# Channel attention over 384 x 384 x 384: VectorE sums 20 rows of a tile and TensorE's last rows wait for it

## The chip, the cores and the metric

One core of one Trainium2 chip. The time is device microseconds of that core. Three runs of the kernel before took 527.71, 527.98 and 530.86 us; their median is 527.98.

## What is computed

`x` is one image of 384 x 384 pixels with 384 channels in bf16 (113.2 MB), `w1d` a single weight. The mean of each channel over all pixels is multiplied by the weight and put through a sigmoid; every pixel is then multiplied by that vector of 384 gates.

```python
g = jnp.einsum("bhwc->bc", x) / (H * W)
s = _sigmoid(g * w1d[0])          # k = 1: the window has one tap
return x * s[:, None, None, :]
```

The image has to be read once and written once, 226.5 MB in all, and the gate of the first pixel depends on the last.

## The kernel before

The kernel doesn't read the image twice. It estimates the gate from the first four rows (`sum_early`, `s_early`), multiplies every tile by that estimate and stores it, while it sums the whole image on the side. At the end it computes the true gate (`s_true`) and compares the two as bf16 bit patterns. Where they differ anywhere (`redo`), a second pass loads, multiplies and stores everything again; otherwise it is skipped. For the reference's data it is skipped.

A "row" is one pixel for each of the 128 partitions: 128 x 384 values. There are 1152 rows, in 18 tiles of `TILE` = 64 rows (6.3 MB). SBUF holds `SLOTS` = 4 tiles; tile k lies in slot k mod 4, so the load of tile k waits until the store of tile k-4 has landed. Loads are issued by SP (some of the first four tiles' by ScalarE), stores by ScalarE. Both kinds of transfer run on the same 16 DMA engines.

A tile's work is split over two engines:

- **TensorE** sums the first 48 rows (`TILE - OWN`) by matmuls with a matrix of ones, 512 columns at a time, so 36 matmuls a tile, into three PSUM banks (`acc` of group 1). This is the loop of `sum_all`: for each tile it waits for the semaphore `ready`, then runs the first `FORE` = 32 rows and signals, then the other 16 and signals again. GpSimd does nothing but relay: when all of a tile's loads have landed it raises `ready` (L119, L467).
- **VectorE** sums the last `OWN` = 16 rows by one `reduce_sum` over the rows (`sum_own`, L338), adds that to `own` (L345), and then multiplies the whole tile in place by `s_early` (`put` and `gate`, L210). The product overwrites what TensorE reads, so it waits for TensorE's signal of that tile. Tile 0's product is cut in two at row `FORE`, so that its first part needs only TensorE's first signal.

The order of the work on each engine is that in which the function calls `plan.op` and `plan.dma`; the class `Planner` adds the semaphore waits from what each operation reads and writes. In the loop over k (L457) come, for each tile from the fifth on: VectorE's sum and product of tile k-4 and its store, then the load of tile k. Before the load of tile 4, ScalarE runs one long activation whose result nobody uses (`pause`, L399), so that this load starts some microseconds after the first store has landed. The last tile is multiplied first, into another slot, and summed afterwards (L474, L475).

At the end `join_own` splits `own` into three bf16 terms, which TensorE sums over the partitions into `acc_own`; `add_banks` adds the PSUM banks together in six VectorE operations; then come the true gate on ScalarE, the comparison, its maximum (`wrong`) and the cast to the integer `redo`. `second_pass` lets SP, ScalarE and VectorE read `redo` from SBUF and branch. After that block ScalarE waits for all 18 stores (L597), two in one instruction.

Of the kernel before, what the change touches and what calls it, by code (L numbers as in the profile page):

```python
# [3 lines left out]
P = 128  # L4
# [151 lines left out]

TILE, SLOTS, EARLY, LEAD, FORE, OWN = 64, 4, 4, 8, 32, 16


PAUSE = 9


def bass_standalone__channel_attn_eca__vision_kernel(
# [10 lines left out]
    def dram(view, r0, n):  # L176
# [4 lines left out]
    w_one = nc.alloc_sbuf_tensor("w_one", [1, 16], BF16)  # L181
    w_scaled = nc.alloc_sbuf_tensor("w_scaled", [P, 2], F32)
    warm = nc.alloc_sbuf_tensor("warm", [P, 2], F32)
    wrong = nc.alloc_sbuf_tensor("wrong", [P, 1], F32)
    redo = nc.alloc_sbuf_tensor("redo", [P, 1], I32)
    total = nc.alloc_sbuf_tensor("total", [P, C], F32)
    zeros = nc.alloc_sbuf_tensor("zeros", [P, 2], BF16)
    own = nc.alloc_sbuf_tensor("own", [P, C], F32)
    part = nc.alloc_sbuf_tensor("part", [P, C], F32)
    terms = nc.alloc_sbuf_tensor("terms", [P, 3 * C], BF16)  # L190
    n_arena = nc.sbuf_bytes_remaining // (2 * C)
    arena = nc.alloc_sbuf_tensor("arena", [P, n_arena * C], BF16)
    acc = [
        [nc.alloc_psum_tensor(f"acc{g}_{i}", [P, WIDE], F32) for i in range(3)]
        for g in range(2)
    ]
    w_all = nc.alloc_psum_tensor("w_all", [P, WIDE], F32)
    acc_own = nc.alloc_psum_tensor("acc_own", [P, WIDE], F32)

    def at(r0, n):  # L200
        assert r0 + n <= n_arena
# [9 lines left out]

    n_tiles = n_rows // TILE
    base = SLOTS * TILE
    assert n_rows % TILE == 0 and base + PAUSE <= n_arena
    assert EARLY % 4 == FORE % 4 == (TILE - OWN) % 4 == 0 and EARLY <= LEAD <= FORE
    last = n_tiles - 1
    ready = nc.alloc_semaphore("ready")

    def slot(k):
        return k % SLOTS * TILE  # L220
# [39 lines left out]
    def add_rows(e, group, column, n, start, stop):  # L260

        n_wide = n * C // WIDE
        all_of = [
            mm(
                e,
                acc[group][i % 3][:, :],
                ones[:],
                arena[:, column + i * WIDE : column + (i + 1) * WIDE],
                start and i < 3,
                stop and i >= n_wide - 3,  # L270
            )
            for i in range(n_wide)
        ]
        return all_of[-1]
# [9 lines left out]
    def nothing(e, bank, start):  # L284

        none = zeros[:, 0:1].broadcast_to([P, WIDE])
        return mm(e, acc[1][bank][:, :], ones[:], none, start, not start)

    def sum_all():

        def one(e, s):
            e.wait_ge(ready, 1).then_inc(ready, -1)  # L292
            for r, n in ((0, FORE), (FORE, TILE - OWN - FORE)):
                add_rows(e, 1, (slot(s) + r) * C, n, False, False).then_inc(
                    plan.sems["tensor"], 1
                )

        def emit(e):
            for i in range(3):
                nothing(e, i, True)  # L300
            rounds = -(-n_tiles // SLOTS)
            some = n_tiles - (rounds - 1) * SLOTS
            with e.Fori(0, rounds) as k:
                for s in range(some):
                    one(e, s)
                if some < SLOTS:
                    with e.If(k < rounds - 1):
                        for s in range(some, SLOTS):
                            one(e, s)
            for i in range(3):  # L310
                done = nothing(e, i, False)
            done.then_inc(plan.sems["tensor"], 1)

        plan.streams["tensor"].append(("block", emit, None))

    def add_banks(group, copy):

        for m, lo, hi in ((0, 0, C), (0, C, WIDE), (1, 0, 256), (1, 256, WIDE),
                          (2, 0, P), (2, P, WIDE)):
            c = (128 * m + lo) % C  # L320
            part = total[:, c : c + hi - lo]
            of = acc[group][m][:, lo:hi]
            if copy and (m, lo) == (0, 0):
                emit = lambda e, part=part, of=of: e.tensor_copy(part, of)  # L324
            else:
                emit = lambda e, part=part, of=of: e.tensor_tensor(  # L326
                    part, part, of, ALU.add
                )
            plan.op("vector", emit, reads=[f"acc{group}", "total"], writes=["total"])

    def sum_own(k):

        r0 = slot(k) + TILE - OWN
        view = at(r0, OWN).rearrange("p (t c) -> p c t", t=OWN)
        to = part if k else own
        plan.op(
            "vector",
            lambda e: e.reduce_sum(to[:], view, axis=mybir.AxisListType.X),  # L338
            reads=rows(r0, OWN),
            writes=["part" if k else "own"],  # L340
        )
        if k:
            plan.op(
                "vector",
                lambda e: e.tensor_tensor(own[:], own[:], part[:], ALU.add),  # L345
                reads=["own", "part"],
                writes=["own"],
            )

    def join_own():  # L350

        for i in range(3):
            term = terms[:, i * C : (i + 1) * C]
            plan.op(
                "vector",
                lambda e, term=term: e.tensor_copy(term, own[:]),  # L356
                reads=["own"],
                writes=[f"term{i}"],
            )
            if i < 2:  # L360
                plan.op(
                    "vector",
                    lambda e, term=term: e.tensor_tensor(  # L363
                        own[:], own[:], term, ALU.subtract
                    ),
                    reads=["own", f"term{i}"],
                    writes=["own"],
                )
        for i in range(3):
            term = terms[:, i * C : (i + 1) * C]  # L370
            plan.op(
                "tensor",
                lambda e, i=i, term=term: mm(
                    e, acc_own[:, :C], ones[:], term, i == 0, i == 2
                ),
                reads=["ones", f"term{i}"],
                writes=["acc_own"],
            )

    def put(place, n, r0, to=None, parts=None):  # L380
        to, i = place if to is None else to, 0
# [11 lines left out]

    def pause(r0):

        to = at(base, PAUSE)
        plan.op(
            "scalar",
            lambda e: e.activation(  # L399
                to, warm[:, 0:1].broadcast_to([P, PAUSE * C]), ACT_F.Sigmoid  # L400
            ),
            reads=["warm"],
            writes=rows(r0, 1) + ["pause"],
        )

    def weight():

# [22 lines left out]
            )  # L430

    plan.op("gpsimd", lambda e: e.memset(warm[:, 0:1], 0.0), writes=["warm"])
    plan.op("vector", lambda e: e.memset(ones[:], 1.0), writes=["ones"])  # L433
    plan.op("gpsimd", lambda e: e.memset(zeros[:], 0.0), writes=["zeros"])
    load(0, TILE, 0, hi=LEAD)
    plan.dma("sync", w_one[0:1, 0:1], w1d.unsqueeze(0), writes=["w_one"])
# [5 lines left out]
    heads = {e: len(plan.streams[e]) for e in ("sync", "scalar")}  # L442
    weight()
    sum_early()
    add_banks(0, copy=True)
    plan.op(
        "scalar",
        lambda e: e.activation(  # L448
# [5 lines left out]
    plan.need("tensor", ["zeros"])  # L454
    sum_all()

    for k in range(n_tiles):  # L457
        if k >= SLOTS:

            for i in range(2) if k == SLOTS else () if k < SLOTS + 2 else (k - SLOTS,):  # L460
                sum_own(i)
                put(slot(i), TILE, row0(i), parts=None if i else (FORE, TILE - FORE))
            if k == SLOTS:
                pause(slot(k))
            load(slot(k), TILE, row0(k), reads=["pause"] if k == SLOTS else ())
        there = rows(slot(k), TILE)
        plan.relay(ready, "gpsimd", "tensor", there, rows(slot(k), FORE), ["acc1"])  # L467
        plan.signals("tensor", rows(slot(k) + FORE, TILE - OWN - FORE), ["acc1"])
    plan.signals("tensor", [], ["acc1"])
    for k in range(n_tiles - SLOTS, last):  # L470
        sum_own(k)
        put(slot(k), TILE, row0(k))

    put(slot(last), TILE, row0(last), slot(n_tiles))  # L474
    sum_own(last)  # L475
    join_own()


    add_banks(1, copy=True)
    plan.op(  # L480
        "vector",
        lambda e: e.tensor_tensor(total[:], total[:], acc_own[:, :C], ALU.add),  # L482
        reads=["acc_own", "total"],
        writes=["total"],
    )
    plan.op(
        "scalar",
        lambda e: e.activation(  # L488
# [12 lines left out]
    )  # L501
    plan.op(
        "vector",
        lambda e: e.reduce_max(wrong[:], total[:], axis=mybir.AxisListType.X),  # L504
        reads=["total"],
        writes=["wrong"],
    )
    plan.op(
        "vector",
        lambda e: e.tensor_copy(redo[:], wrong[:]),  # L510
        reads=["wrong"],
        writes=["redo"],
    )
    checked = (plan.sems["vector"], plan.count["vector"])
# [5 lines left out]
    for k, n in enumerate(split(n_rows, half)):  # L520
        place = above + k % 2 * half
        again.dma("sync", at(place, n), dram(x_rows, r0, n), writes=rows(place, n))
        again.op(
            "vector",
            gate(place, place, n, s_true),
            reads=rows(place, n),
            writes=rows(place, n),
# [31 lines left out]
    with nc.Block() as block:  # L559
# [18 lines left out]
        @block.vector  # L578
        def _(e):
            plan.emit("vector", e)  # L580
            second_pass("vector", e)

        @block.scalar
        def _(e):
# [7 lines left out]
        @block.gpsimd  # L592
        def _(e):
            plan.emit("gpsimd", e)

    for token in plan.final:
        nc.scalar.wait_ge(*token)  # L597
# [28 lines left out]
```

## Time and profile before

The profiled execution took 527.94 us, with a span of 526.5 us from the first to the last instruction.

| | |
|---|---|
| runs | 527.71, 527.98, 530.86 us |
| profiled execution, its span | 527.94, 526.5 us |
| VectorE busy | 440.0 us (84%), 78 instructions |
| TensorE busy | 180.0 us (34%), 648 matmuls |
| ScalarE, GpSimd busy | 5.8 us, 0.3 us |
| DMA | 226.51 MB, mean 430 GB/s over the span |
| VectorE products (L210) | 17 of 12.95 us, two of 6.56 us |
| VectorE sums of 16 rows (L338) | 18, mean 10.5 us |
| VectorE adds of 128x384 f32 (L345) | 17 of 0.56 us |
| a load of one tile, issue to landing | 41.8 us (median) |
| a store of one tile, issue to landing | 49.9 us (median) |

A page of a profile gives each engine's busy time over the whole span, and the same in 40 slices of 13.2 us, one digit a slice, in tenths. A line of the timeline gives start and duration in us, engine, line of the code, operation, output and input with partitions and elements, and in brackets how long the engine stood idle before it and what released it. A line of the waits says who waited for whom: the total in us, the number of times, and the longest. A busy share says little by itself: an engine that has time to spare costs nothing, and one that is busy beside a slower one doesn't either.

### The profile page before, as it was taken

The numbers are of one execution on the slowest core, as the hardware profiler recorded it, in microseconds if no ns is written. First come the engines' busy times: TensorE is split into PE (matmuls) and PEld (weight loads), VectorE is DVE, ScalarE is ACT, GpSimd is POOL, SyncE is SP. The second block draws the span as 40 slices with busy tenths as digits, with TensorE's granted clock in tenths as the row PEclk, the third lists the DMA queues.
The fourth block names the chain that finished last, engine by engine and source line by source line (L and its number), as shares of the span: only waits on it lengthen the run. The fifth ranks groups of instructions, "written<-read, shape, count | busy, mean of one in ns | idle before, by whom it ended". The sixth has DMA issues, their size and how long they took to land.

```text
span 526.5 us, 902 instructions
## 1 busy us (share of the span) xinstructions
PE 180.0 (34%) x648; PEld 0.2 (0%) x2; DVE 440.0 (84%) x78; ACT 5.8 (1%) x5; POOL 0.3 (0%) x6
## 2 busy tenths in 40 slices
PE   2255752043240707061422506070513315070701
PEld 0000000000000000000000000000000000000000
DVE  1869999999996978969696969789696969698795
ACT  1000020000000000000000000000000000000000
POOL 0000000000000000000000000000000000000000
PEclk9996967558585858567575858576675858585765
DMA  9999999999999999999999999999999999999998
GB/s 375 433 459 405 418 448 448 418 418 467 429 418 418 467 429 418 429 459 426 418 429 459 426 418 441 445 429 418 448 437 429 418 459 429 426 418 459 429 426 359
DMA packets 5620, 226.51 MB, mean 430 GB/s; under 512 B 626, under 2 KB 626, under 8 KB 754
## 3 DMA queue, kind: packets, MB, share of 16 engines
q10 hardware_dynamic: 3024, 122.29, 53.7%
q1 hardware_dynamic: 2594, 104.20, 46.0%
q14 instruction: 2, 0.02, 0.0%
HBM read 113.25 MB, written 113.25 MB: 430 GB/s over the span
## 4 chain that ended last, share of the span: by engine, by line
DMA 42%; another core or an unknown queue 27%; DVE 21%; issue 7%; SPq 0%; ACT 0%; DVEq 0%
DMA arena<-in_x_dram 24%; DMA out_dram<-arena 18%; DVE part L338 12%; DVE arena L210 7%; DVE own L345 1%; DVE total L326 0%; SPq L109 0%; DVE own L363 0%; DVE terms L356 0%; ACT arena L488 0%; DVE total L496 0%; DVE total L482 0%; DVE wrong L504 0%; DVE total L324 0%
## 5 line engine op out<-in xcount | busy, mean ns | idle before, releaser
L248 PE MATMUL acc<-arena,ones 128*128 128x512 bf16 x637 | 176.1, 441 | 312.2 <-PEq L292 310.8
L210 DVE TENSOR_TENSOR arena<-arena,s_early 128x24576 bf16<-128x24576 bf16 (+1 forms) x19 | 233.2, 12278 | 11.5 <-PE acc L248 6.5
L338 DVE TENSOR_REDUCE part<-arena 128x384 f32<-128x6144 bf16 x17 | 179.2, 10539 | 56.9 <-DMA arena<-in_x_dram 56.9
L338 DVE TENSOR_REDUCE own<-arena 128x384 f32<-128x6144 bf16 x1 | 10.4, 10435 | 0.6 <-DMA arena<-in_x_dram 0.6
L345 DVE TENSOR_TENSOR own<-own,part 128x384 f32<-128x384 f32 x17 | 9.5, 558 | 0.6
L425 DVE TENSOR_SCALAR w_scaled<-w_all 128x1 f32<-128x1 f32 x2 | 0.2, 152 | 8.0 <-PE w_all L416 8.0
L248 PE MATMUL acc_own<-terms,ones 128*128 128x384 bf16 x3 | 1.4, 479 | 15.3 <-DVE terms L356 15.3
L488 ACT ACTIVATE arena<-total,w_scaled 128x384 bf16<-128x384 f32 x1 | 0.6, 615 | 440.3 <-DVE total L482 440.3
L326 DVE TENSOR_TENSOR total<-total,acc 128x128 f32<-128x128 f32 (+2 forms) x10 | 3.9, 393 | 0.3
L399 ACT ACTIVATE arena<-warm 128x3456 bf16<-128x3456 f32 x1 | 3.1, 3082 | 61.9 <-DMA out_dram<-arena 61.9
L416 PE MATMUL w_all<-w_one,ones 1*128 1x1 bf16 x1 | 0.2, 158 | 9.3 <-DMA w_one<-in_w1d_dram 9.3
L248 PE MATMUL acc<-zeros,ones 128*128 128x512 bf16 x6 | 2.3, 507 | 0.0
L324 DVE COPY total<-acc 128x384 f32<-128x384 f32 x2 | 1.1, 554 | 1.2 <-PE acc L248 1.2
L410 ACT ACT_TABLE_LOAD x1 | 1.3, 1283 | 2.3 <-issue 2.3
L433 DVE MEMSET ones<- 128x128 bf16 x1 | 0.2, 165 | 1.3 <-PEq L611 1.3
L363 DVE TENSOR_TENSOR own<-own,terms 128x384 f32<-128x384 f32 x2 | 1.1, 559 | 0.1
L356 DVE CAST terms<-own 128x384 bf16<-128x384 f32 x3 | 1.1, 359 | 0.1
L496 DVE TENSOR_TENSOR total<-arena,s_early 128x384 f32<-128x384 uint16 x1 | 0.6, 558 | 0.7 <-ACT arena L488 0.7
L448 ACT ACTIVATE s_early<-total,w_scaled 128x384 bf16<-128x384 f32 x1 | 0.6, 614 | 9.8 <-DVE total L326 9.8
L482 DVE TENSOR_TENSOR total<-total,acc_own 128x384 f32<-128x384 f32 x1 | 0.6, 554 | 0.1
L246 PE MATMUL acc<-arena,ones 128*128 128x512 bf16 x1 | 0.6, 608 | 0.0
L504 DVE TENSOR_REDUCE wrong<-total 128x1 f32<-128x384 f32 x1 | 0.6, 553 | 0.0
(10 smaller groups left out, 1.2 us busy)
## 6 DMA issues: line engine op xcount, KB each, us to landing
out_dram<-arena ACTq DMA_DIRECT2D x18, 6144.0 KB, 49.9
arena<-in_x_dram SPq DMA_DIRECT2D x16, 6144.0 KB, 41.8
arena<-in_x_dram ACTq DMA_DIRECT2D x2, 3072.0 KB, 41.5
arena<-in_x_dram ACTq DMA_DIRECT2D x1, 2688.0 KB, 14.0
arena<-in_x_dram SPq DMA_DIRECT2D x1, 2688.0 KB, 21.4
arena<-in_x_dram SPq DMA_DIRECT2D x1, 768.0 KB, 7.8
w_one<-in_w1d_dram SPq DMA_DIRECT2D x1, 0.0 KB
```

What stands on the lines that cost most here:

```text
L210: return lambda e: e.tensor_tensor(to_v, v, s_b, ALU.mult)
L246: loaded.append(e.matmul(bank, weights, moving, start=start, stop=stop))
L248: return e.add_instruction(mybir.InstMatmult(name=nc.get_next_instruction_name(), engine=mybir.EngineType.PE, ins=[e.lower_ap(moving), e.l ...
L324: emit = lambda e, part=part, of=of: e.tensor_copy(part, of)
L326: emit = lambda e, part=part, of=of: e.tensor_tensor(part, part, of, ALU.add)
L338: lambda e: e.reduce_sum(to[:], view, axis=mybir.AxisListType.X),
L345: lambda e: e.tensor_tensor(own[:], own[:], part[:], ALU.add),
L356: lambda e, term=term: e.tensor_copy(term, own[:]),
L363: lambda e, term=term: e.tensor_tensor(own[:], own[:], term, ALU.subtract),
L399: lambda e: e.activation(to, warm[:, 0:1].broadcast_to([P, PAUSE * C]), ACT_F.Sigmoid),
L410: lambda e: e.activation(warm[:, 1:2], warm[:, 0:1], ACT_F.Sigmoid),
L448: lambda e: e.activation(s_early[:], total[:], ACT_F.Sigmoid, scale=w_scaled[:, 0:1]),
```

## The change

Six things are changed together.

1. `OWN` goes from 16 to 20 and `FORE` from 32 to 40. VectorE sums 20 rows of each tile; TensorE sums 44, of which 40 (30 matmuls) after `ready`.
2. TensorE's last 4 rows (3 matmuls) wait for a new semaphore, `summed`, which VectorE's sum of that tile raises. VectorE's product then needs one wait, for TensorE, which covers the reading of both engines.
3. A tile's sum isn't added to `own` at once. It goes to one of six places above the slots (`part(i)`, f32); after every fourth tile (4, 8, 12, 16) one `reduce_sum` over five places joins them, behind that tile's product. At the end the remaining two are joined into `own`.
4. The three PSUM banks of a group are one tensor, and one `reduce_sum` over its four pieces of 384 columns (`total_of`) takes the place of six operations. The three terms of `own` are added by TensorE into the first of these banks, so `acc_own` and its addition go.
5. The second pass multiplies on GpSimd, so GpSimd reads `redo` and VectorE no longer does. The maximum is written as an integer directly, without the cast. The memset of `ones` is on GpSimd.
6. The pause is three activations of 1152 columns rather than one of 3456.

```diff
-TILE, SLOTS, EARLY, LEAD, FORE, OWN = 64, 4, 4, 8, 32, 16
-PAUSE = 9
+TILE, SLOTS, EARLY, LEAD, FORE, OWN = 64, 4, 4, 8, 40, 20
+PARTS = 6
+PAUSE, PAUSES = 3, 3
...
-    acc = [
-        [nc.alloc_psum_tensor(f"acc{g}_{i}", [P, WIDE], F32) for i in range(3)]
-        for g in range(2)
-    ]
+    acc = [nc.alloc_psum_tensor(f"acc{g}", [P, 3 * WIDE], F32) for g in range(2)]
...
+    summed = nc.alloc_semaphore("summed")
...
         def one(e, s):
-            e.wait_ge(ready, 1).then_inc(ready, -1)
-            for r, n in ((0, FORE), (FORE, TILE - OWN - FORE)):
+            for of, r, n in ((ready, 0, FORE), (summed, FORE, TILE - OWN - FORE)):
+                e.wait_ge(of, 1).then_inc(of, -1)
                 add_rows(e, 1, (slot(s) + r) * C, n, False, False).then_inc(
                     plan.sems["tensor"], 1
                 )
...
-            for i in range(3):
-                done = nothing(e, i, False)
-            done.then_inc(plan.sems["tensor"], 1)
+            for i in (1, 2):
+                nothing(e, i, False)
...
-    def add_banks(group, copy):
...
+    def total_of(group):
+        view = acc[group][:, :].rearrange("p (t c) -> p c t", c=C)
+        plan.op(
+            "vector",
+            lambda e: e.reduce_sum(total[:], view, axis=mybir.AxisListType.X),
+            reads=[f"acc{group}"],
+            writes=["total"],
+        )
+
+    def part(i, n=1):
+        return at(base + 2 * i, 2 * n).bitcast(F32)
...
     def sum_own(k):
         r0 = slot(k) + TILE - OWN
         view = at(r0, OWN).rearrange("p (t c) -> p c t", t=OWN)
-        to = part if k else own
+        i = free[0]
+        free[0] += 1
+        reads, writes = rows(r0, OWN), part_rows(i)
+        for token in plan._needs(reads, writes):
+            plan._wait("vector", token)
+        plan.streams["vector"].append(
+            (
+                "op",
+                lambda e: e.reduce_sum(part(i), view, axis=mybir.AxisListType.X),
+                summed,
+                1,
+            )
+        )
+        plan._record(all_summed[k], reads, writes)
+        kept.append(i)
+
+    def join_parts(to=None):
+        lo, n = min(kept), len(kept)
+        assert sorted(kept) == list(range(lo, lo + n))
+        i = 0 if lo else PARTS - 1
+        view = part(lo, n).rearrange("p (t c) -> p c t", c=C)
+        out = part(i) if to is None else to[:]
         plan.op(
             "vector",
-            lambda e: e.reduce_sum(to[:], view, axis=mybir.AxisListType.X),
-            reads=rows(r0, OWN),
-            writes=["part" if k else "own"],
+            lambda e: e.reduce_sum(out, view, axis=mybir.AxisListType.X),
+            reads=part_rows(lo, n),
+            writes=["own"] if to is not None else part_rows(i),
         )
-        if k:
-            plan.op(
-                "vector",
-                lambda e: e.tensor_tensor(own[:], own[:], part[:], ALU.add),
-                reads=["own", "part"],
-                writes=["own"],
-            )
+        kept[:], free[0] = [i], 1
...
-                lambda e, i=i, term=term: mm(
-                    e, acc_own[:, :C], ones[:], term, i == 0, i == 2
-                ),
+                lambda e, term=term: mm(e, acc[1][:, :C], ones[:], term, False, False),
...
-        to = at(base, PAUSE)
+        to, of = terms[:, : PAUSE * C], warm[:, 0:1].broadcast_to([P, PAUSE * C])
+        for i in range(PAUSES):
...
-    plan.op("vector", lambda e: e.memset(ones[:], 1.0), writes=["ones"])
+    plan.op("gpsimd", lambda e: e.memset(ones[:], 1.0), writes=["ones"])
...
+    def put_tile(k):
+        sum_own(k)
+        put(slot(k), TILE, row0(k), parts=None if k else (FORE, TILE - FORE))
+        if len(kept) == PARTS - 1:
+            join_parts()
...
         plan.signals("tensor", rows(slot(k) + FORE, TILE - OWN - FORE), ["acc1"])
-    plan.signals("tensor", [], ["acc1"])
+        all_summed.append((plan.sems["tensor"], plan.count["tensor"]))
...
     put(slot(last), TILE, row0(last), slot(n_tiles))
     sum_own(last)
+    join_parts(own)
     join_own()
-    add_banks(1, copy=True)
-    plan.op(
-        "vector",
-        lambda e: e.tensor_tensor(total[:], total[:], acc_own[:, :C], ALU.add),
...
+    total_of(1)
...
-        lambda e: e.reduce_max(wrong[:], total[:], axis=mybir.AxisListType.X),
+        lambda e: e.reduce_max(redo[:], total[:], axis=mybir.AxisListType.X),
...
         again.op(
-            "vector",
+            "gpsimd",
             gate(place, place, n, s_true),
...
         def _(e):
             plan.emit("vector", e)
-            second_pass("vector", e)
...
         @block.gpsimd
         def _(e):
             plan.emit("gpsimd", e)
+            second_pass("gpsimd", e)
```

## The prediction

> **What bounds the kernel now.** I read the share of the DMA engines first, then the waits, then VectorE's own timeline, then the end. From the page, VectorE's and the DMA's rows over 40 slices:
>
> ```profile
> DVE  1869999999996978969696969789696969698795
> ...
> DMA  9999999999999999999999999999999999999998
> ```
>
> The DMA engines are never below nine tenths. VectorE has idle slices only from about 140 us on. The waits say for what, and what the loads wait for:
>
> ```profile
> DVE part L338 <- DMA arena<-in_x_dram: 56.9, 13, 5.3
> ```
>
> ```profile
> SPq L109 <- DMA out_dram<-arena: 364.1, 13, 28.8
> ```
>
> Thirteen times VectorE waits some 5 us for a tile to land, and a load is issued when the store that frees its slot has landed. So the middle is bound by bytes: 226.5 MB at 430 GB/s is the whole span, and a tile takes 29.0 us. VectorE's work for one tile, where it waits for nothing:
>
> ```profile
> 92.32 10.41 DVE L338 TENSOR_REDUCE part<-arena 128x384 f32<-128x6144 bf16 x1
> ...
> 102.76 0.56 DVE L345 TENSOR_TENSOR own<-own,part 128x384 f32<-128x384 f32 x1
> 103.24 12.95 DVE L210 TENSOR_TENSOR arena<-arena,s_early 128x24576 bf16<-128x24576 bf16 x1
> ...
> 116.11 10.51 DVE L338 TENSOR_REDUCE part<-arena 128x384 f32<-128x6144 bf16 x1
> ```
>
> From start to start 23.8 us: sum 10.44, add 0.48, product 12.87 (the records overlap by 0.08). VectorE has 5.2 us a tile to spare, and none of its work but the first tile's and the last's shows in the time. The end:
>
> ```profile
> 489.92 12.96 DVE L210 TENSOR_TENSOR arena<-arena,s_early 128x24576 bf16<-128x24576 bf16 x1 [5.04 <-DMA arena<-in_x_dram]
> ...
> 502.79 10.41 DVE L338 TENSOR_REDUCE part<-arena 128x384 f32<-128x6144 bf16 x1
> ...
> 521.28 0.15 DVE L510 CAST redo<-wrong 128x1 int32<-128x1 f32 x1
> ```
>
> ```profile
> L597 ACTq EVENT_SEMAPHORE  x9: 38/38/38, 523.2 to 526.4; - x9
> ```
>
> The last load lands at 489.9, its store is issued at 502.9 and lands 23.5 us later, at 526.4. Beside it VectorE ends the sum: the flag is written at 521.43, the engines read it and leave the block by 523.2, and ScalarE's nine waits for the stores begin; the trace's records have the eighth at 524.1, and only the ninth waits, until 526.4. So the flag's chain needs about 2.7 us after `redo` and has 2.3 us to spare. **Anything that makes VectorE's chain end more than 2.3 us later sets the time.** Span 526.5, run 527.94: 1.5 us lie around it, and that run stands 0.04 under the median.
>
> **What the Trainium skill says.** "VectorE: DVE Perf Modes", The perf-mode tier table: a reduce has only the 1x mode, a bf16 product reaches 2x. The trace agrees: the product takes 0.53 ns an element, the sum (10.42 - 0.15)/6144 = 1.67 ns (0.15 is what the one-column operations cost). The contiguous reduce of L504 takes (0.55 - 0.15)/384 = 1.05. "Advanced Engine Details and Errata", Memory Cachelines: touching another 16-byte line at each access costs; that fits 1.67 against 1.05, as the sum steps a row (768 bytes) at a time. "TensorE: Matmul & The Clock Gate", Part 1: after some 3.4 us idle the array runs at half clock, 427 against 216 ns for 512 columns. The trace agrees: granted clock 0.50 in 92 to 100 us where TensorE idles. "DMA: Bandwidth & Descriptors", Issuing engines are not separate DMA queues: both queues share 16 engines. The trace agrees: 434 GB/s in 461 to 490 us with loads and stores, 442 to 457 in 490 to 505 with stores alone.
>
> **The change, part by part.**
> *Rows.* VectorE sums 20 rows for 16: 7680 x 1.67 ns + 0.15 = 13.0 us, 2.56 more a tile. TensorE has 33 matmuls for 36; it idles half the time, worth nothing by itself.
> *The new wait.* The last 3 matmuls wait for VectorE's sum, and the product, which overwrites the tile, waits for them. Before, all 36 were done when the sum was (9.3 to 10.4 us against 10.5), so this wait was free. Now VectorE stands still for the hop to TensorE and three matmuls. The nearest row is the opening:
>
> ```profile
> 9.37 0.61 PE L246 MATMUL acc<-arena,ones 128*128 128x512 bf16 x1
> ...
> 9.77 1.06 PE L248 MATMUL acc<-arena,ones 128*128 128x512 bf16 x2
> ...
> 10.87 0.56 DVE L324 COPY total<-acc 128x384 f32<-128x384 f32 x1 [1.17 <-PE acc L248]
> ```
>
> Three matmuls at half clock, until the VectorE copy that waits for them starts: 1.50 us; with 0.1 for the hop there (load landing to TensorE's start is 0.13) 1.6. At full clock 3 x 0.22 + 0.2 = 0.85, the lower bound. I take 1.6: with VectorE as the pace, TensorE does the next tile's 30 matmuls during the product (some 8.5 us of 12.9) and then idles 17 us. Behind the waiting matmuls stand the next tile's 30, which have that product's time; who waits for the three is the product, and behind it the store and the load into that slot.
> *Joins.* 17 adds of 0.48 go. After tiles 4, 8, 12 and 16 a reduce of 5 parts (1920 f32, in steps of 1536 bytes), at the end one of 2. Not shown by the trace for f32: at 1.05 ns 2.2 and 0.95 us, at 1.67 ns 3.4 and 1.45. A third reading, that the sum is 16 cycles plus a fixed cost for each of its 384 outputs, gives 6.1 and 4.9 (and 12.0 for the sum of 20 rows). I take 1.67, since the steps are long too.
> *PSUM totals.* Copy and five adds (2.7 us) and the add of `acc_own` (0.6) become one reduce of 1536: 1.75, 2.75 or 5.7 us by the same three readings; I take 2.75. The first total's difference is hidden: the first product waits for TensorE at 31.08, `s_early` is there at 14.2.
> *FORE 40.* The first product waits for 30 matmuls, not 24: 6 x 0.22 = 1.3 us, at 32.4; tile 0's store goes out at 45.3, not 44.1.
> *Pause in three, memset of `ones` and second pass on GpSimd, the dropped cast.* The pause delays only the load of tile 4, which lands at 112 us and is wanted at 128. `ones` is wanted at 9.3. GpSimd reads the flag in VectorE's place (0.93 us there; unknown on GpSimd, -0.3 to +1.5, taken as 0). The cast is worth 0.15. SP's and ScalarE's transfers stay the same ones in the same order.
>
> **The sum.** One tile on VectorE becomes 13.0 + 1.6 + 12.9 = 27.5 us, with a join each fourth tile 28.3: under 29.0, but the cover is nearly gone, and VectorE starts late. Loads of the first tiles are there early (tile 4 at 112 us), and VectorE, done with tile 0 at 45.3, wants tile 5 at about 159 where it landed at 141; it never again meets a late load. Tiles 1 to 16: 45.3 + 16 x 27.5 + 4 x 3.4 = 498.9. The last load is there at 490, so the last product ends at 511.8, 9 us later than before. Then sum 13.0, wait for TensorE 1.6, join 1.45, casts and subtractions 2.35, two matmuls 0.9, total 2.75, ScalarE 0.7, the compare and the maximum 1.15: `redo` at 535.7. Flag 2.7: span 538.4, and 1.5 around it: **539.9 us**, 2.3% more. The last store, issued at 511.8, lands by 526.5: the DMA queue no longer sets the end. What is late next is VectorE's chain from 45 us on.
>
> **Rivals.**
> *Cover holds (not slower).* If the three matmuls run at full clock (0.85), tiles 1 to 16 end at 45.3 + 16 x 26.75 + 13.6 = 486.9, before the last load at 490. Then only the tail counts: 502.9 + 23.2 + 2.7 + 1.5 = 530.3, +0.4%. It decides from the point where the tile falls under 26.9. For it: records from 62.5 to 66 show that the clock stays up some 4 us after the last matmul. Against it: the idle time is 17 us once VectorE paces.
> *F32 reduces at 1.05 ns:* 4 x 1.2 + 0.5 + 1.0 less: 533.6, just on the edge.
> *Fixed cost per output:* 17 x 1.0 less for sums, 4 x 2.7 + 3.4 + 3.0 more for reduces: 540.
> *Stores starve.* A store is issued some 2 us before or after the previous one lands (20 us before, now). Then one queue works alone; 490 to 522 us shows no loss of rate, so I allow 5 us: 545.
> *Faster* than 1% would need fewer bytes or a higher rate; the DMA's 226.5 MB leave 2 us at most.
> *It doesn't do what it says:* if the product didn't wait for the three matmuls, it would be the first rival with 0: 529.4.
>
> **Numbers.** Forecast 0.47, cover holds or no wait 0.18, fast f32 0.20, cost per output 0.09, starved 0.04, faster 0.02. About 1% (533.3) is what a measurement of this kernel tells from no change. Half of the fast-f32 case is above it: slower 0.70, same 0.28, faster 0.02. Range 529.5 to 544.
>
> **What would show it.** The sum at 13.0; each product starting 1.6 after its sum, with TensorE as releaser; reduces of 128x1920 at 3.4; VectorE's waits for loads gone after tile 1; the last product near 499; the last of ScalarE's final waits no longer the late one. Waits of VectorE for loads that stay, or a gap under 1 us, would make the prediction wrong.

## The result, and the profile after

The changed kernel takes 536.74 us (median of six runs, 536.35 to 537.68), against 528.14 before: a ratio of 1.0156, with a 95% interval of 1.0134 to 1.0178. It is 8.6 us slower. The ratios here and below are the recorded ones; they differ from the quotients of the medians by up to 0.0014. The profiled execution took 536.56 us, with a span of 535.0.

From the page of the kernel after, the busy tenths of VectorE and of the DMA engines in 40 slices of 13.4 us:

```profile
DVE  1969898989898989899998989898989898989995
...
DMA  9999999999999999999999999999999999999992
```

From 40 us on VectorE is busy eight or nine tenths of every slice but the last; the deeper gaps that began at 140 us are gone. The DMA engines still look full, but in the last slice they are nearly done, and VectorE is not. The waits, in total, number of times and longest, name the new one:

```profile
DVE arena L206 <- PE acc L245: 29.7, 17, 4.3
...
DVE arena L353 <- DMA arena<-in_x_dram: 1.8, 1, 1.8
```

Before, 13 of VectorE's sums waited for a load, 57 us in all. Now one does, at tile 0, and 17 products wait for TensorE: tile 0's, which waited before too (6.5 us then, 4.3 now), and 16 new ones, 25.4 us together. One tile on the timeline (start, duration, engine, line):

```profile
185.33 12.97 DVE L353 TENSOR_REDUCE arena<-arena 128x384 f32<-128x7680 bf16 x1
...
198.41 8.67 PE L245 MATMUL acc<-arena,ones 128*128 128x512 bf16 x33 [18.70 <-PEq L295]
199.89 12.96 DVE L206 TENSOR_TENSOR arena<-arena,s_early 128x24576 bf16<-128x24576 bf16 x1 [1.59 <-PE acc L245]
212.76 12.97 DVE L353 TENSOR_REDUCE arena<-arena 128x384 f32<-128x7680 bf16 x1
```

The sum takes 12.97 us, then VectorE stands for 1.59 until TensorE has done three matmuls (the line of 33 is those three and the next tile's 30), then comes the product: 27.43 us from sum to sum. TensorE had been idle for 18.7 us before these three, and the clock granted to it while they run, from 198.4 to 199.9 us, is 0.50. The end of VectorE's chain:

```profile
497.47 12.95 DVE L206 TENSOR_TENSOR arena<-arena,s_early 128x24576 bf16<-128x24576 bf16 x1
510.34 12.97 DVE L353 TENSOR_REDUCE arena<-arena 128x384 f32<-128x7680 bf16 x1
...
529.22 1.76 DVE L322 TENSOR_REDUCE total<-acc 128x384 f32<-128x1536 f32 x1 [1.00 <-PE acc L245]
...
532.25 0.55 DVE L529 TENSOR_REDUCE redo<-total 128x1 int32<-128x384 f32 x1
```

The last product starts at 497.5, 7.6 us later than before, and no load holds it: it follows the last join at once, and the last load had landed at 488.4, by its landing records (489.9 before). So the loads weren't late. `redo` is written at 532.8, 11.4 us later than before. ScalarE's nine waits for the stores, by their line:

```profile
L616 ACTq EVENT_SEMAPHORE  x9: 38/38/38, 534.1 to 535.0; - x9
```

None of them waits now. They pass within a microsecond, because the last store had landed 17.8 us after its issue at 510.4, at 528.3. The program ends when VectorE's chain and the reading of the flag end.

### The profile page after: what moved, and what is told of

It is laid out like the page before. It is cut to its first block, busy times and chain, and to the rows that moved or that the text cites. A ratio compares the mean times of both kernels' runs of the same rounds, so it can differ in the third digit from the quotient of the medians.

```text
span 535.0 us, 843 instructions
## 1 busy us (share of the span) xinstructions
PE 177.9 (33%) x607; PEld 0.2 (0%) x2; DVE 487.0 (91%) x53; ACT 6.2 (1%) x7; POOL 0.5 (0%) x7
## 3 DMA queue, kind: packets, MB, share of 16 engines
q1 hardware_dynamic: 2594, 104.20, 45.3%
## 5 line engine op out<-in xcount | busy, mean ns | idle before, releaser
L245 PE MATMUL acc<-arena,ones 128*128 128x512 bf16 x596 | 173.4, 459 | 340.5 <-PEq L295 340.5
L206 DVE TENSOR_TENSOR arena<-arena,s_early 128x24576 bf16<-128x24576 bf16 (+2 forms) x19 | 233.3, 12283 | 29.7 <-PE acc L245 29.7
L353 DVE TENSOR_REDUCE arena<-arena 128x384 f32<-128x7680 bf16 x18 | 233.7, 12981 | 2.1 <-DMA arena<-in_x_dram 1.8
L370 DVE TENSOR_REDUCE arena<-arena 128x384 f32<-128x1920 f32 x4 | 13.6, 3395 | 0.0
L322 DVE TENSOR_REDUCE total<-acc 128x384 f32<-128x1536 f32 x2 | 3.5, 1757 | 2.2 <-PE acc L245 2.2
L427 ACT ACTIVATE terms<-warm 128x1152 bf16<-128x1152 f32 x3 | 3.5, 1162 | 62.7 <-DMA out_dram<-arena 62.7
L245 PE MATMUL acc<-terms,ones 128*128 128x384 bf16 x3 | 1.4, 479 | 1.6 <-DVE terms L382 1.6
L243 PE MATMUL acc<-arena,ones 128*128 128x512 bf16 x1 | 0.6, 607 | 0.0
```

Source lines behind the costliest of these rows:

```text
L206: return lambda e: e.tensor_tensor(to_v, v, s_b, ALU.mult)
L243: loaded.append(e.matmul(bank, weights, moving, start=start, stop=stop))
L245: return e.add_instruction(mybir.InstMatmult(name=nc.get_next_instruction_name(), engine=mybir.EngineType.PE, ins=[e.lower_ap(moving), e.l ...
L322: lambda e: e.reduce_sum(total[:], view, axis=mybir.AxisListType.X),
L353: lambda e: e.reduce_sum(part(i), view, axis=mybir.AxisListType.X),
L370: lambda e: e.reduce_sum(out, view, axis=mybir.AxisListType.X),
```

## The experiments

The theory: each part of the change is hidden by itself, and together they make VectorE's chain from 45 us on longer than the transfers. The first rival says that the wait costs by itself, the second that the rows or the joins do, the third that the transfers became slower. The kernel before was timed beside every one of these runs, at 527.9 to 528.1 us (medians).

**The wait alone, on the kernel before.** Sixteen rows and an add for each tile stay; the last four of TensorE's 48 rows wait for the sum.

```diff
-            for r, n in ((0, FORE), (FORE, TILE - OWN - FORE)):
+            for r, n in ((0, FORE), (FORE, TILE - OWN - FORE - 4), (TILE - OWN - 4, 4)):
+                if n == 4:
+                    e.wait_ge(summed, 1).then_inc(summed, -1)
```

> The kernel before (16 rows, an add for each tile) with the new wait alone: the last 4 of TensorE's 48 rows wait for VectorE's sum. VectorE's tile becomes 23.85 + 1.6 = 25.4 us, under the 29.0 of the transfers: hidden but for the tail, where 1.6 us fit into the 2.3 that the flag has to spare: 528.1 us. Rival (the wait is a cost of its own wherever it stands): 17 x 1.6 = 27 us more, or at least a few us; over 531.

Measured: 528.10 us, ratio 1.0000 (0.9986 to 1.0014). VectorE waits for TensorE 17 times, 18.9 us in all, and the time doesn't move. From the waits and the timeline of this kernel:

```profile
DVE part L346 <- DMA arena<-in_x_dram: 43.0, 12, 4.2
DVE own L355 <- PE acc L250: 18.9, 17, 1.6
```

```profile
461.38 10.01 PE L250 MATMUL acc<-arena,ones 128*128 128x512 bf16 x33 [17.65 <-PEq L294]
471.93 0.81 PE L250 MATMUL acc<-arena,ones 128*128 128x512 bf16 x3 [0.53 <-PEq L297]
472.77 0.56 DVE L355 TENSOR_TENSOR own<-own,part 128x384 f32<-128x384 f32 x1 [0.96 <-PE acc L250]
```

Most of what the new wait takes, the wait for the next load gives back (43 us in place of 57). In the tile shown the three matmuls follow the other 33 after 0.5 us, with a granted clock of 1.00, so the gap is 0.96, not 1.59. In the tail, where VectorE waits for nothing else, it is 1.59 at a granted clock of 0.50; `redo` is written there 2.0 us later than before, at 523.4, and the time doesn't show it.

**The rows alone, on the kernel before.** `OWN` 20 and `FORE` 40, nothing else.

> The kernel before with 20 rows on VectorE and FORE 40, nothing else. A tile takes VectorE 26.4 us, hidden under 29.0; the tail's sum is 2.55 us longer against 2.3 to spare: 528.4 us. Rival (the rows are the cost): 17 x 2.55 = 43 us on a chain that is paced by VectorE, or any time over 531.

Measured: 528.9 us, ratio 1.0009 (0.9985 to 1.0033). The waits of VectorE's sums for loads fall from 57 us to 18:

```profile
DVE part L338 <- DMA arena<-in_x_dram: 18.0, 9, 2.6
```

The median is 0.8 us above that of the kernel before, which the interval doesn't tell from nothing.

**All but the wait.** The changed kernel, where `sum_own` is a plain operation and TensorE runs through its 33 matmuls.

> The changed kernel, but TensorE sums all 44 rows without waiting for VectorE's sum; the product waits for both. If VectorE's own chain sets the pace from 45 us on, a tile takes it 12.98 + 12.87 = 25.85 us, and 44.6 + 16 x 25.85 + 4 x 3.46 = 472 lies before the last load (490): VectorE waits for loads again in the last tiles, the last product starts at 490, the flag is done by about 526.0 and the last store lands at 526.4: 527.9 us. Rival (20 rows and the joins alone fill VectorE, or they slow the transfers): no VectorE wait for loads, 533 us or more.

Measured: 529.19 us, ratio 1.0008 (0.9984 to 1.0033). Rows and joins together leave VectorE waiting eight times for loads (the profile is of the slowest of the twelve runs, 531.75 us):

```profile
DVE arena L350 <- DMA arena<-in_x_dram: 20.3, 8, 3.3
```

So the rows alone, the wait alone, and all parts but the wait have medians at most 1.1 us above that of the kernel before, with intervals that include no change. The joins weren't run alone. The wait costs on top of the rest.

**The wait kept, its price taken away.** All 33 matmuls stand ahead of the wait; one matmul of one column of zeros behind it carries the signal.

```diff
+            add_rows(e, 1, (slot(s) + FORE) * C, TILE - OWN - FORE, False, False)
+            e.wait_ge(summed, 1).then_inc(summed, -1)
+            mm(
+                e, acc[1][:, 2 * WIDE : 2 * WIDE + 1], ones[:], zeros[:, 0:1], False, False
+            ).then_inc(plan.sems["tensor"], 1)
```

> The changed kernel with its wait kept, but all 33 matmuls stand ahead of it, and only one matmul of one column of zeros behind it, which carries the signal. If the 1.59 us are three matmuls at half clock (3 x 0.43) and a hop, the gap between sum and product falls to 0.3 to 0.4 us, a tile to 26.2, and 44.6 + 16 x 26.2 + 13.8 = 478 lies before the last load: 528.0 us. Rival (the hop there and back is the cost): the gap stays above 1.2 us and the time at 532 us or more.

Measured: 528.60 us, ratio 1.0005 (0.9981 to 1.0029). From its timeline:

```profile
153.10 12.98 DVE L357 TENSOR_REDUCE arena<-arena 128x384 f32<-128x7680 bf16 x1
166.20 0.16 PE L245 MATMUL acc<-zeros,ones 128*128 128x1 bf16 x1 [19.90 <-PEq L299]
166.40 12.96 DVE L206 TENSOR_TENSOR arena<-arena,s_early 128x24576 bf16<-128x24576 bf16 x1 [0.32 <-PE acc L245]
```

The whole way there and back takes 0.32 us. The other 1.27 us of the gap are the three matmuls, and without them behind the wait the time can't be told from that of the kernel before.

**The wait made longer.** `FORE` 36 puts six matmuls behind the wait.

> The changed kernel with FORE 36: 8 rows, so 6 matmuls behind the wait and not 3. If VectorE's chain is the pace in all 17 tiles, each pays 3 x 0.43 = 1.28 us more: the last product starts at 44 + 16 x 28.7 + 13.8 = 517, and the time is 557 us. Rival (the transfers set the pace and the change costs in the tail alone): 1.3 us more, 538.

Measured: 557.96 us, ratio 1.0562 (1.0541 to 1.0583), 21.2 us more than the changed kernel. The gap is 2.87 us, 1.28 more, as in tile 1:

```profile
60.30 12.96 DVE L206 TENSOR_TENSOR arena<-arena,s_early 128x24576 bf16<-128x24576 bf16 x1 [2.87 <-PE acc L245]
```

It is so at each of the 16 tiles and once more in the tail: 17 x 1.28 = 21.8, less 0.2 that the smaller `FORE` saves at tile 0 and 0.2 of a shorter wait for the PSUM total; the spans differ by 21.4. Every microsecond that the wait adds to VectorE's chain shows in the time.

**The clock.** Here 48 matmuls of zeros run in each tile, from the end of the previous product on.

```diff
+                if r == 0:
+                    e.wait_ge(begun, 1).then_inc(begun, -1)
+                    for i in range(48):
+                        mm(e, acc[1][:, 2 * WIDE :], ones[:], none, False, False)
```

> The changed kernel with 48 matmuls of zeros on TensorE in every tile, begun when the product before has ended, so that the clock is up when the last three come. If half clock is what makes the gap 1.59 us, it falls to 0.85, a tile to 26.7, and 44.6 + 16 x 26.7 + 13.8 = 485.6 lies before the last load: 528 us, with a gap of 0.8 to 0.9. Rival (the clock doesn't matter): gap 1.6, 536.7 us; or the zeros run over the end of the sum and the gap grows.

Measured: 538.87 us, ratio 1.0201 (1.0180 to 1.0221); the expected time was missed by 11 us, and half of the reason for it held. In six of the 16 tiles the gap is 0.96; in the good tile below the granted clock is 1.00 (337 to 340 us) and the three matmuls take 0.81 us, where they took 1.44 at 0.50. But the zeros also get in the way. From its timeline, a good tile and a late one:

```profile
338.69 0.81 PE L246 MATMUL acc<-arena,ones 128*128 128x512 bf16 x3 [1.86 <-PEq L297]
339.53 12.96 DVE L206 TENSOR_TENSOR arena<-arena,s_early 128x24576 bf16<-128x24576 bf16 x1 [0.96 <-PE acc L246]
...
472.04 10.61 PE L246 MATMUL acc<-zeros,ones 128*128 128x512 bf16 x47
482.50 0.81 PE L246 MATMUL acc<-arena,ones 128*128 128x512 bf16 x3
483.34 12.96 DVE L206 TENSOR_TENSOR arena<-arena,s_early 128x24576 bf16<-128x24576 bf16 x1 [3.98 <-PE acc L246]
```

In the last three tiles the 30 matmuls start late, as their load lands late, and the zeros run over the end of the sum: gaps of 2.5, 2.3 and 4.0 us. In tile 0 the second half of the product waits 2.9 us for them. Over tiles 1 to 16 the gaps add up to 24.1 us, against 25.4 in the changed kernel, and tile 0 takes more than that back. So half clock is 0.63 us of the 1.59 (0.96 against it, and 1.44 against 0.81), and keeping the clock up this way is no remedy.

**The joins done twice.**

> The changed kernel with each of the four joins done twice over. If all of a join lies on VectorE's chain, 4 x 3.46 = 13.8 us more: 550.6 us. Rival (VectorE has time to spare around the joins, as a tile of 28.3 us on average is under 29.0): under 540.

Measured: 550.36 us, ratio 1.0422 (1.0392 to 1.0452): 13.6 us more than the changed kernel. That is what four more joins take (4 x 3.46 = 13.8).

**Adds in place of joins.** After each product VectorE adds the part to a running sum, and nothing is joined every fourth tile.

> The changed kernel with an add of 0.48 us after each tile's product in place of the four joins of 3.46. A tile takes 12.98 + 1.59 + 12.87 + 0.48 = 27.9 us, so tiles 1 to 16 end at 44.6 + 16 x 27.9 = 491, 6 us earlier than with joins, just behind the last load: about 530 us. Rival (the joins lie in time that VectorE would wait anyway): 536.7.

Measured: 535.47 us (532.61 to 539.47 in four runs), ratio 1.0129 (1.0063 to 1.0195). The expected 530 was missed. An add costs 0.65 us from start to start here and not 0.48, which makes 2.7 of the 5.5 us. The rest isn't VectorE's; it waits for loads again, 1.1 us at the last sum but one and 2.0 at the last product. Final waits of ScalarE in the profiled execution (537.85 us):

```profile
L629 ACTq EVENT_SEMAPHORE  x9: 38/38/38, 533.3 to 536.3; - x9
```

`redo` is written at 532.05, so the flag's chain alone would end at 534.3; the last store lands at 536.3, ten microseconds later than in the kernel before, though no byte was added. Each transfer of the image has 16 landing records, one for each share of it, and it has landed with the last of them. The second last store's 16 shares come in from 511.0 to 521.8 us here, from 510.3 to 513.8 in the changed kernel, and from 510.5 to 511.7 before. In the kernel with adds three of a store's 16 shares come late, in every store from 155 us on. The cause stays open. One guess, too few transfers in the queues, doesn't suffice: from 100 to 490 us 3.1 transfers are outstanding on average before, 2.7 here and 2.5 in the changed kernel, which has the fewest of the three and far less of this than the kernel with adds.

The four runs fall in two pairs, 532.61 and 533.10, and 537.85 and 539.47. Without its 3.1 us of waiting for loads, the profiled one would have its flag done at 531.2 and take 532.7 us. That is an estimate from its trace, and the lower pair lies there. By this estimate rows and wait together, with an add for each tile as before, already cost some 5 us on VectorE's chain; the joins bring the rest (3.8 by the next experiment).

**Adds in place of joins where VectorE paces clearly** (`FORE` 36).

> Six matmuls behind the wait, and the add of 0.65 us after each product in place of the joins: VectorE paces so clearly here that the transfers can't set the end. Against 558.0 with joins: 16 x 0.65 - 4 x 3.46 - 0.4 = -3.8, so 554.2 us. Rival (what kept the kernel with adds above 530 us is VectorE's and not the transfers'): no gain, 558.

Measured: 554.19 us, ratio 1.0495 (1.0464 to 1.0525), 3.8 us less than with joins. So joins and adds are worth on VectorE's chain what their durations say. With the waits for loads and the late last store in the trace above, it was the transfers that kept the kernel with adds up.

**The price of a reduce.** Sixteen reduces to 384 outputs at the end of the changed kernel; only their durations count.

> The changed kernel with sixteen more reduces on VectorE at its end, for their durations; its own time says nothing. Known so far: 5 f32 parts take 1.68 ns an element, 2 take 1.05, PSUM with 4 takes 1.05, 16 and 20 bf16 rows 1.67. If the long step between terms is the cost, all reduces with terms apart take 1.6 to 1.7 from some number of terms between 3 and 5 on, and the same numbers of terms side by side take 1.05. If it is a fixed cost per output, side by side and apart are alike, and the cost per element falls with more terms.

Durations in us, from the trace:

```
terms for each output      2     3     4     5     6     8    20
f32, a row apart        0.95  1.47  2.75  3.39  4.03  5.31
bf16, a row apart       0.95  1.35  2.74  3.38        5.30 12.98
f32, side by side       0.95              2.15
bf16, side by side                        2.15              8.15
```

Side by side an element costs 1.05 ns, whatever the number of terms; so there is no fixed cost per output. A row apart it costs the same up to three terms in bf16 (1.15 in f32) and 1.67 to 1.69 from four on. The step between terms is the cost, but only when four or more rows are read in turn. No other steps were measured (a row is 768 bytes in bf16, 1536 in f32), and why the cost sets in at four stays open.

## Why the prediction was right

*The bound before.* That VectorE had 5.2 us a tile to spare is borne out by the rows alone, the wait alone and all but the wait: ratios of 1.0000 to 1.0009, with intervals up to 1.0033. That the flag's chain had 2.3 us to spare fits the wait alone, where `redo` came 2.0 us later at no cost.

*The rows.* 13.0 us were forecast, 12.97 measured.

*The wait.* The working put it at 1.6 us; it is 1.59. That VectorE's pace leaves TensorE at half clock was the step that decided between the forecast and the first rival, and the kernel with the wait alone shows both sides: 0.96 where the transfers pace, 1.59 where VectorE does. The bound of 0.85 for full clock was 0.11 too low.

*The joins.* 3.4 us were taken for five parts, 3.38 to 3.43 measured (3.46 from start to start). The joins done twice and the adds show that they lie on the chain. The rate was in part luck: the reason given, that the steps are long, holds as well for the join of two and for the PSUM total, where it gave the wrong rate. What separates them in SBUF is the number of terms.

*The sum.* Tiles 1 to 16 were to end at 498.9; the last product starts at 497.5. The reasoning that a tile of 28.3 us under a transfer of 29.0 isn't hidden, since VectorE begins late and never catches up, held: there is no wait for a load after tile 0.

*What was off.* The forecast run was 539.9, against 536.6 for the profiled one; 3.4 us of span, in six terms. The rise was put at 11.9 us and is 8.6. The PSUM total took 1.76 and not 2.75 (-1.0): the rate of 1.67 ns was carried over to PSUM, where four terms apart run at 1.05 ns. The join of two took 0.96 and not 1.45 (-0.5), as two terms run at 1.05 too. The start was 44.6 and not 45.3 (-0.7): the first product started at 31.63, 0.55 us later than before, where six more matmuls had been put at 1.3. The tile was 27.43 and not 27.5 (-1.1 over 16). The flag took 2.25 and not 2.7 (-0.45): the engines read `redo` in 0.46 to 0.48 us, in place of 0.83 to 0.93. The joins took 0.2 more in all. The sum of these is -3.5, within rounding of the 3.4.

*The rivals.* "Fast f32" was right for PSUM and for the join of two and wrong for the four joins, which weigh most. "Cost per output" is refuted by the reduces side by side. "Cover holds" is what happens as soon as the three matmuls leave the path (528.6). "Stores starve" didn't set the time of the changed kernel: VectorE did, and the last store had landed 6.7 us before the end. But it isn't empty: in the profiled execution of the kernel with adds the transfers end late and set the time. That the bytes "leave 2 us at most" for a faster kernel isn't shown: it takes the mean rate of this kernel, 430 GB/s, for the most that is possible, and 490 to 500 us, with stores alone, shows 457.

## What to carry to other kernels

Time to spare on an engine is one purse: changes that stay hidden in it when made apart can cost 8.6 us together, so add up all that they take from the same engine, with the waits, and not only per tile but from the moment at which the engine starts. A wait on another engine costs what stands between it and its signal, so put the work ahead of the wait and leave the smallest instruction behind it: here 0.32 us in place of 1.59. None of these versions is shown to be faster than the kernel before, whose DMA engines are busy nine tenths or more in all but the last of 40 slices.

## What was not expected of the hardware

A VectorE reduce whose terms lie a row apart has two rates, with a step between three and four terms: 1.05 to 1.15 ns an element up to three, 1.67 to 1.69 from four on, in SBUF, for bf16 and f32 alike (steps of 768 and 1536 bytes). That each access touches another line of memory, the reason that the prediction named, doesn't tell them apart: with two and three terms each access steps a row as well. From PSUM, four f32 terms 1536 bytes apart run at 1.05 ns (1.76 us less 0.15, for 1536).

A transfer's 16 shares, which from 150 us on land within 1.3 to 2.6 us of each other in the kernel before, can drift apart: with adds in place of joins one store's came in from 473 to 489 us. No byte was added and there was no moment without a transfer outstanding, and yet the last store landed 10 us late. It differs from one execution to another: in the changed kernel the shares come in within 4.3 us at most, and in the kernel with the sixteen reduces, which is the same up to 527 us, within 1.7.
